# Seven products in the second layer of the last block of the second MLP, with GpSimd summing its weights

## The chip, the cores and the metric

The kernel runs on one core of a Trainium2 chip. The core has a matrix engine (TensorE, PE in the profile), three engines for elementwise work (VectorE, DVE; ScalarE, ACT; GpSimd, POOL) and a queue engine (SyncE, SP) that issues most transfers. The metric is the time of one execution in device microseconds, lower is better; the time before is the median of three runs.

## The reference

The program is three stages on 2304 tokens (4 sequences of 576) of 512 numbers. First comes attention with random features, then a mixer MLP (over tokens, then over channels), and then the stage that the change is in:

```python
X = np.fft.fft(np.fft.fft(x, axis=1), axis=2)
u = x + np.real(X)
un = (u - mean(u)) / np.sqrt(var(u) + 1e-06)      # over the 512 channels
return u + np.maximum(un @ w_ch1, 0.0) @ w_ch2    # 512 -> 2048 -> 512
```

All of it is in float32. The kernel keeps that precision with three matmuls in a reduced format (fp32r) for each product: each operand is split into a high part and a rest, and high x high, high x rest and rest x high are summed in PSUM. So every weight lies in memory twice, as a high part and as a rest (`kept`), and every activation is split by two operations, a copy on ScalarE (high) and a subtraction on VectorE (rest).

## The kernel before, in words

The second MLP runs over three blocks of token tiles of 128 rows: `PLAIN` (4 tiles), and the two of `PAIRED` with 6 and 8 tiles. The change is in the last one, c = 1, with 8 tiles, which are two halves of 4 tiles, that is of 512 tokens.

Layer one of a paired block (`paired_block`, first loop) takes the hidden units in 8 pairs of slabs (p_ = 0 to 7), each slab 128 hidden units. For a pair, the two token halves and the two halves of the 512 inputs make a 2 x 2 block product, and the kernel forms it with seven products (P1 to P7, each six matmuls of 512 columns in `product`, L1519) in place of eight, by sums of weights and of activations that are made beforehand. The products go into two PSUM banks X and Y in turn; VectorE and ScalarE combine them to four results: the hidden values of the two token halves for the two slabs. Those of the first token half are split at once and used; those of the second wait in SBUF (`held`).

Layer two multiplies the hidden values with `kept[2, p_]` in the plain way: `downs` gives 12 matmuls of 512 columns for a slab and a token half of 4 tiles. Within pass p_ the list `todo` holds the 24 matmuls of pass p_ - 1 for the first token half, and they are run in four groups between the products, so that TensorE has work while the other engines combine. After the eight passes the second token half follows, slab by slab (16 slabs, `part` splits a slab two ahead).

The order of every engine's work is the order in which the program issues it; a wait on one instruction holds what is behind it on the same engine. Weights come through `Slots` (six buffers w0 to w5 of 512 KB, `ffw`): SP fetches them in the order of the list `flow`, a fetch is issued when a buffer comes free, some five fetches ahead. `side` spreads other work (transforms and norms of later tiles) over TensorE's steps; by the last block it is empty. The sums of the first layer's weights are made the same way earlier (`sum_pairs`, on VectorE, stored by GpSimd's queue). Results are added to the rows in SBUF and sent out by `put_out` (L1275). `reopen` (L1507) runs once in block 0, when the transform's buffers are free, and opens the pool `g2` in their place. `prepare_ff` (L1347) makes the last block's activations and their sums between the slabs of block 0's second token half.

## Time and profile before

| | |
|---|---|
| median of three runs | 934.48 us (934.14 to 936.88) |
| the profiled execution | 934.46 us |
| its span in the trace | 932.7 us |
| TensorE busy | 923.9 us, 99% |
| VectorE, ScalarE, GpSimd busy | 638.1, 305.6, 134.4 us |
| granted TensorE clock | 0.999 |
| DMA | 214.36 MB, mean 230 GB/s |

The span is the time from the first to the last instruction; what the execution takes beyond it is start and end of the program. Busy time counts an engine's instructions, and overlapping matmuls count once. An engine that is busy for nearly the whole span need not be at its best rate: how far apart matmuls of one kind start says more, and a timeline shows that. The last block's passes begin at 760.8 us.

### The profile page before, as it was taken

How to read it: one execution, taken by the hardware profiler on the slowest of the kernel's cores; microseconds unless marked ns; L12 is line 12 of the kernel's file. 1: busy time of each engine (PE TensorE's matmuls, PEld its weight loads, DVE VectorE, ACT ScalarE, POOL GpSimd, SP SyncE). 2: the span in 40 equal slices, each digit the busy share in tenths (PEclk: the TensorE clock that was granted, in tenths of full speed). 3: DMA queues.
4: the chain of work that ended last, by engine and by line, in shares of the span. 5: the costliest groups of instructions: out<-in, count | busy, mean ns of one | idle time of the engine just before them, and what ended most of it. 6: DMA issues, size and time to landing. Idle time of an engine off the chain costs nothing.

```text
span 932.7 us, 13693 instructions
## 1 busy us (share of the span) xinstructions
PE 923.9 (99%) x5174; PEld 812.1 (87%) x5174; DVE 638.1 (68%) x1231; ACT 305.6 (33%) x697; POOL 134.4 (14%) x133
## 2 busy tenths in 40 slices
PE   8999999999999999999999999999999999999998
PEld 8999999988889888888888888889999888888886
DVE  6987999896775788876796795536666764333432
ACT  5886777742121222221222222221111251111220
POOL 3353444221211122101020001000000000000000
PEclk9999999999999999999999999999999999999999
DMA  8765564688996687595197958247765657566452
GB/s 278 231 213 177 180 220 160 242 305 318 329 420 259 240 297 268 197 337 189 54 371 298 327 190 289 84 160 247 242 218 184 216 197 229 181 199 196 159 193 100
DMA packets 61825, 214.36 MB, mean 230 GB/s; under 512 B 5568, under 2 KB 6208, under 8 KB 48064
## 3 DMA queue, kind: packets, MB, share of 16 engines
q1 hardware_dynamic: 51104, 153.52, 47.2%
q0 software_dynamic: 10512, 59.84, 17.6%
q8 instruction: 41, 0.67, 0.3%
q14 instruction: 24, 0.20, 0.1%
q10 hardware_dynamic: 144, 0.13, 0.0%
HBM read 167.20 MB, written 42.47 MB: 225 GB/s over the span
## 4 chain that ended last, share of the span: by engine, by line
PE 95%; DVE 2%; ACT 1%; DMA 1%; issue 0%; SPq 0%; DVEq 0%; ACTq 0%
PE H L786 20%; PE A L1538 16%; PE A L912 16%; PE H L1525 14%; PE A L1297 5%; PE A L511 5%; PE N L587 3%; PE H L545 3%; PE A L570 2%; PE A L690 2%; PE S L1094 2%; PE A L677 1%; PE S L1107 1%; PE S L690 1%; PE H L677 1%; PE S L677 1%
## 5 line engine op out<-in xcount | busy, mean ns | idle before, releaser
L786 PE MATMUL H<-uh,w 128*128 128x512 f32 (+1 forms) x608 | 188.0, 375 | 0.0
L786 PEld LDWEIGHTS H<-uh,w 128*128 128x128 f32 x608 | 111.9, 188 | 19.6
L874 ACT ACTIVATE hh<-H 128x512 fp32r<-128x512 f32 (+1 forms) x76 | 42.9, 565 | 237.8 <-PE H L786 232.8
L786 PE MATMUL H<-ul,w 128*128 128x512 f32 (+1 forms) x304 | 113.5, 373 | 0.4 <-DVE ul L773 0.4
L912 PE MATMUL A<-hh,w 128*128 128x512 f32 (+1 forms) x480 | 109.6, 371 | 0.0
L1525 PE MATMUL H<-b,w1t 128*128 128x384 f32 (+1 forms) x480 | 104.2, 363 | 0.0
L1525 PEld LDWEIGHTS H<-b,w1t 128*128 128x128 f32 x480 | 87.4, 188 | 11.5 <-DVE b L1338 0.4
L912 PEld LDWEIGHTS A<-hh,w 128*128 128x128 f32 x480 | 83.5, 189 | 14.6
L875 DVE SCALAR_TENSOR_TENSOR hl<-H,hh 128x512 fp32r<-128x512 f32 (+1 forms) x76 | 49.0, 645 | 61.7 <-ACT hh L874 61.5
L1538 PE MATMUL A<-w2t,hx 128*128 128x512 f32 x336 | 81.9, 392 | 0.0
L529 ACT ACTIVATE f<-A,mx 128x128 f32<-128x128 f32 x240 | 69.7, 397 | 23.3 <-DVE mx L525 22.8
L1538 PEld LDWEIGHTS A<-w2t,hx 128*128 128x128 f32 x336 | 62.5, 188 | 12.7
L786 PEld LDWEIGHTS H<-ul,w 128*128 128x128 f32 x304 | 57.3, 188 | 10.2 <-DVE ul L773 0.8
L912 PE MATMUL A<-hl,w 128*128 128x512 f32 (+1 forms) x240 | 59.2, 368 | 0.0
L912 PEld LDWEIGHTS A<-hl,w 128*128 128x128 f32 x240 | 42.6, 188 | 7.6
L525 DVE TENSOR_REDUCE mx<-A 128x4 f32<-128x512 f32 x70 | 47.5, 681 | 1.0 <-ACT f L529 0.9
L1538 PE MATMUL A<-w2t,hy 128*128 128x512 f32 x192 | 46.8, 389 | 0.0
L1538 PEld LDWEIGHTS A<-w2t,hy 128*128 128x128 f32 x192 | 36.0, 188 | 7.5
L545 PE MATMUL H<-v,f 128*128 128x65 f32 x320 | 40.2, 270 | 1.2 <-ACT f L533 0.8
L545 PEld LDWEIGHTS H<-v,f 128*128 128x128 f32 x320 | 38.9, 191 | 1.9 <-ACT f L533 1.0
L360 DVE SCALAR_TENSOR_TENSOR cvo<-cvy,cvo 128x1024 int32<-128x1024 int32 (+2 forms) x32 | 39.7, 1239 | 0.5
L364 DVE SCALAR_TENSOR_TENSOR cvo<-cvo,stg 128x1024 f32<-128x1024 int32 (+2 forms) x32 | 39.9, 1247 | 0.0
(278 smaller groups left out, 1712.4 us busy)
## 6 DMA issues: line engine op xcount, KB each, us to landing
w<-kept SPq DMA_DIRECT2D x50, 1024.0 KB, 7.3
w2t<-kept SPq DMA_DIRECT2D x55, 512.0 KB, 4.2
w1t<-kept SPq DMA_DIRECT2D x48, 512.0 KB, 4.6
stg<-in_wff_dram POOLq DMA_DIRECT2D x16, 1024.0 KB, 6.9
kept<-cvo POOLq DMA_DIRECT2D x13, 1024.0 KB, 7.4
stg<-in_wch_dram SPq DMA_DIRECT2D x9, 1024.0 KB, 6.4
kept<-cvo POOLq DMA_DIRECT2D x16, 512.0 KB, 8.1
sw<-kept POOLq DMA_DIRECT2D x8, 1024.0 KB, 7.8
```

The costliest lines, as they stand in the source:

```text
L364: dve.scalar_tensor_tensor(out=st["l"].bitcast(F32), in0=st["l"], scalar=2.0 ** 32, in1=st["lw"].bitcast(U32), op0=ALU.mult, op1=ALU.add)
L511: pe.matmul(out=pj[:, p_ * 256:p_ * 256 + 256], lhsT=a[:, c, :], rhs=w, start=(n == 0), stop=(n == 2), skip_group_check=True)
L525: dve.tensor_reduce(out=mx, in_=p4, axis=AX.X, op=ALU.max, negate=True)
L529: act.activation(out=f[:, hh], in_=p4[:, hh], func=AF.Exp, bias=mx[:, hh])
L545: pe.matmul(out=kvp[b, g][:, hh * 65:hh * 65 + 65], lhsT=ft["k", i, g][:, hh, :], rhs=src["v", i, int(off > 0)][:, 4 * g + hh, :], start=( ...
L786: pe.matmul(out=hb[:, 0:n], lhsT=w(a, kk), rhs=u[:, kk, 0:n], start=(c == 0), stop=(c == 11))
L874: act.activation(out=hh, in_=hb[:, 0:n], func=AF.Relu)
L875: dve.scalar_tensor_tensor(out=hl, in0=hb[:, 0:n], scalar=0.0, in1=hh, op0=ALU.max, op1=ALU.subtract)
L912: pe.matmul(out=acc[i][:, 0:cols], lhsT=a[:, cs], rhs=v, start=(n == 0 and c_ == 0), stop=(n == NCH - 1 and c_ == 2))
L1297: pe.matmul(out=acc[t], lhsT=a[:, t * 128:t * 128 + 128], rhs=w, start=(n == 0 and c_ == 0), stop=(n == NFF - 1 and c_ == 2))
L1525: pe.matmul(out=to, lhsT=w[:, a, cs], rhs=v[:, q], start=(start and n == 0), stop=(n == 5), skip_group_check=True)
L1538: pe.matmul(out=acc[t], lhsT=h[n // 2][:, t * 128:t * 128 + 128], rhs=w[:, n % 2], start=(begins and n == 0), stop=(ends and n == 2))
```

## The change

Layer two of the last block is formed with seven products as well. Its 2 x 2 block product has the two token halves on one side, the two halves of the 512 outputs on the other, and sums over the two slabs of a pair; so a matmul has 256 columns in place of 512, and a product is 12 of them.

- New weights: for each pair, `sums_of_second` loads `kept[2, p]` into SBUF, adds its two slabs and forms four sums or differences of 256 columns on GpSimd, copies the high part on ScalarE, subtracts the rest on GpSimd, and stores both as `kept[4, p]` from GpSimd's queue. The loads, sums and output have one buffer each (tags z0, z1, z2). `split(p)` (copy, rest, store, then the add of the next pair) is called at slabs 3 and 10 of block 0's second half for pairs 0 and 1, and in pass p_ of the last block for pair p_ + 2.
- Passes: the pass combines its products to values of seven operands. Three of the seven products of layer two (`a11`, `cd`, `f2_`) are put off to the next pass as before, 36 matmuls of 256 columns into three accumulators of two banks each. The values for the other four (K12, K3, K4, K22) stay in SBUF in `store`, 32 buffers of 128 x 512.
- After the passes, 32 steps of 12 matmuls take those four products, one after the other, over the eight pairs. Each accumulator is copied to SBUF between two of its uses (`snap`), and the copies are added to the rows in pieces of 256 columns.
- Fetches: of `kept[2, p]` and `kept[4, p]` in pieces of 256 columns, 256 or 512 KB per buffer.

```diff
--- before.py
+++ after.py
@@ -1468,16 +1468,31 @@
         for p_ in range(NP):
             due = due or [None, None]
             flow += [(1, p_, 0), due[0], (1, p_, 1), (1, p_, 2), due[1], (1, p_, 3)]
-            due = [(2, p_, 0), (2, p_, 1)]
+            due = [(5, p_, 0), (4, p_, 0)] if c else [(2, p_, 0), (2, p_, 1)]
         flow += due
+        if c:
+            flow += [(6, i, k) for i in range(4) for k in range(NP // 2)]
+            continue
         rest = [(2, p_, s_) for p_ in range(NP - 1, -1, -1) for s_ in (1, 0)]
         flow += rest[:-2]
         due = rest[-2:]
-    flow += due
...
+        if k > 3:
+            t = pl_.tile([128, 2, 2, 256], F32R, tag=tag, name="w3t")
+            v = t.bitcast(F32)
+            if k == 5:
+                sync.dma_start(out=v[:, 0], in_=kept[2, p_][:, :, 0:256])
+            elif k == 4:
+                sync.dma_start(out=v, in_=kept[4, p_][:, 0:4:3])
+            else:
+                for m in range(2):
+                    q = 2 * i + m
+                    sync.dma_start(out=v[:, m], in_=kept[4, q][:, (1, 2)[p_ // 2]] if p_ % 2 else
+                                   kept[2, q][:, :, 512 + 128 * p_:768 + 128 * p_])
+            return t
         if k == 2:
             t = pl_.tile([128, 2, 512], F32R, tag=tag, name="w2t")
             sync.dma_start(out=t.bitcast(F32), in_=kept[2, p_][:, :, i * 512:i * 512 + 512])
@@ -1489,7 +1504,7 @@
         return t
 
     def made(x):
-        return ((2, x[1]) if x[0] == 2 else (3, x[1])) in whole
+        return {1: (3, x[1]), 2: (2, x[1]), 4: (4, x[1]), 5: (2, x[1]), 6: (4, NP - 1)}[x[0]] in whole
 
...
@@ -1512,9 +1527,45 @@
         hx = xp.tile([128, 6 * n0], F32R, tag="x2", name="hx")
         ring.append([hx[:, n * n0:n * n0 + n0] for n in range(6)])
         hbuf.append([hx[:, n * n1:n * n1 + n1] for n in range(4)])
-        ring.append(hbuf[1])
-        v = [held5[:, n * n1:n * n1 + n1] for n in range(7)]
-        held.append(v + [g2.tile([128, n1], F32, name=f"t3_{n}") for n in range(2 * NP - len(v))])
+        store = [held5[:, n * n1:n * n1 + n1] for n in range(7)]
+        held.append(store + [g2.tile([128, n1], F32, name=f"t3_{n}") for n in range(4)])
+        sums_of_second(g2)
+    def sums_of_second(g2):
+        def load(p):
+            t = g2.tile([128, 2, 1024], F32, tag="z0", name="zw")
+            pool.dma_start(out=t, in_=kept[2, p])
+            return t
+        ws, ys = [], []
+        def add(p):
+            w = ws.pop(0)
+            y = g2.tile([128, 1024], F32, tag="z1", name="zy")
+            ys.append(y)
+            pool.tensor_tensor(out=y, in0=w[:, 0], in1=w[:, 1], op=ALU.add)
+            if p + 1 < NP:
+                ws.append(load(p + 1))
+            v = y.rearrange("p (c n) -> p c n", c=4)
+            for to, a, b in ((0, 1, 0), (1, 3, 1), (3, 3, 0), (2, 2, 3)):
+                pool.tensor_tensor(out=v[:, to], in0=v[:, a], in1=v[:, b], op=ALU.subtract)
+        def split(p):
+            y = ys.pop(0)
+            o = g2.tile([128, 2, 1024], F32R, tag="z2", name="zo")
+            act.copy(out=o[:, 0], in_=y)
+            pool.tensor_tensor(out=o[:, 1], in0=y, in1=o[:, 0], op=ALU.subtract)
+            kept[4, p] = dram.tile([128, 4, 2, 256], F32, name="kept4")
+            keep(pool, kept[4, p], o)
+            whole.add((4, p))
+            if p + 1 < NP:
+                add(p + 1)
+        ws.append(load(0))
+        add(0)
+        tmp["split"] = split
 
...
@@ -1552,9 +1603,6 @@
 
     def paired_block(c, todo, uses, after):
 
-        if c:
-            hy = fp.tile([128, 4 * n1], F32R, tag="t2_5", name="hy")
-            hbuf[1] += [hy[:, n * n1:n * n1 + n1] for n in range(4)]
...
@@ -1636,19 +1684,198 @@
                 run(mats)
                 ffw.used()
                 side.step(S_US)
+                if n in (3, 10):
+                    side.until(lambda: "split" in tmp, side.lead)
+                    tmp["split"](n // 7)
             else:
                 left += mats
         return left, 1, lambda: finish(c, 1, acc)
 
+    def last_block(todo, uses, after):
+        c, g2 = 1, right["n"]
+        hy = fp.tile([128, 4 * n1], F32R, tag="t2_5", name="hy")
+        hy = [hy[:, n * n1:n * n1 + n1] for n in range(4)]
+        parts = [hy[:2], hbuf[1][2:], hbuf[1][:2], hy[2:]]
+        sa, ub, vc, cd = temps(c)
+        left = [g2.tile([128, n1], F32, tag="un", name="ku", bufs=8) for _ in range(8)]
+        store = held[1] + left[:6]
+        f11, f2_ = left[6:]
+        kx = xu.tile([128, 4, n1], F32, tag="x2", name="kx", padded_shape=[128, 4, S])
+        store += [kx[:, n] for n in range(4)]
+        spare_ = []
+        def more():
+            ky = xp.tile([128, 4, n1], F32, tag="x2", name="ky", padded_shape=[128, 4, S])
+            z1 = g2.tile([128, 2, n1], F32, tag="z1", name="kz1")
+            z0 = g2.tile([128, 4, n1], F32, tag="z0", name="kz0")
+            z2 = g2.tile([128, 4, n1], F32, tag="z2", name="kz2")
+            v = [t[:, n] for t, m in ((ky, 4), (z1, 2), (z0, 4), (z2, 4)) for n in range(m)]
+            n = 4 * NP - len(store)
+            store.extend(v[:n])
+            spare_.extend(v[n:])
+        def kept_(p_, i):
+            return store[4 * p_ + i]
+        K12, K3, K4, K22 = range(4)
...
+        by_part = [(t, n) for n in range(3) for t in range(4)]
+        first = len(todo) // 2
+        late = None
+        for p_ in range(NP):
+            X, Y = [bank("H")[:, 0:n1] for _ in range(2)][::(1, -1)[p_ % 2]]
+            a11 = parts[p_ % 2]
+            w = ffw.get((1, p_, 0))
+            product(c, X, w[:, 0], P1, True)
+            act.copy(out=sa, in_=X)
+            product(c, Y, w[:, 1], P6, True)
+            combine(ub, Y, sa, ALU.add)
+            if late:
+                late()
+            ffw.used()
+            side.step(S_US)
+            run(todo, first // 2)
+            if p_ + 2 < NP:
+                tmp["split"](p_ + 2)
+            w = ffw.get((1, p_, 1))
+            product(c, X, w[:, 0], P2, False)
+            relu_parts(a11, X)
+            act.activation(out=f11, in_=X, func=AF.Relu)
+            product(c, Y, w[:, 1], P5, True)
+            combine(vc, Y, ub, ALU.add)
+            side.step(S_US)
+            run(todo, first - first // 2)
+            ffw.used(1 + uses)
+            w = ffw.get((1, p_, 2))
+            product(c, X, w[:, 1], P7, True)
+            combine(kept_(p_, K22), X, vc, ALU.add)
+            relu(kept_(p_, K22))
+            product(c, Y, w[:, 0], P3, False)
+            combine(vc, Y, ub, ALU.add)
+            relu(vc)
+            combine(kept_(p_, K3), f11, vc, ALU.subtract)
+            combine(cd, vc, kept_(p_, K22), ALU.add)
+            combine(f2_, cd, f11, ALU.subtract)
+            ffw.used()
+            side.step(S_US)
+            run(todo, len(todo) // 2)
+            two(parts[2], cd)
+            w = ffw.get((1, p_, 3))
+            product(c, X, w[:, 0], P4, False)
+            combine(kept_(p_, K12), X, ub, ALU.add)
+            relu(kept_(p_, K12))
+            side.step(S_US)
+            run(todo)
+            ffw.used(1 + uses)
+            two(parts[3], f2_)
+            late = lambda p_=p_: combine(kept_(p_, K4), kept_(p_, K12), f2_, ALU.subtract)
+            uses = 1
+            if p_ == 0:
+                after()
+                more()
+                acc1, acc2 = [[bank("A") for _ in range(2)] for _ in range(2)]
+                acc3 = [bank("S") for _ in range(2)]
+                first = 12
...
+            b, e = p_ == 0, p_ + 1 == NP
+            todo += (mats(acc1, a11, weights((5, p_, 0), 0), b, e, by_part)
+                     + mats(acc3, parts[2], weights((4, p_, 0), 0), b, e, by_part)
+                     + mats(acc2, parts[3], weights((4, p_, 0), 1), b, e, by_part))
+        late()
+        chain = [(K12, acc1), (K3, acc2), (K4, acc3), (K22, acc2)]
+        steps = [(i, p_) for i in range(4) for p_ in range(NP)]
+        def part(n):
+            i, p_ = steps[n]
+            h = parts[n % 4]
+            two(h, kept_(p_, chain[i][0]))
+            return h
...
+        m1, m6, m5, m8 = (sa, ub), (vc, cd), spare_[0:2], (spare_[2], f11)
+        at = {0: [lambda: snap(acc3, m5)], 1: [lambda: snap(acc2, m6)], 8: [lambda: snap(acc1, m8)],
+              16: [lambda: snap(acc2, m6)], 24: [lambda: snap(acc3, m5)]}
...
+        spread(2, adds(m5, 1, 256))
+        spread(3, adds(m6, 0, 256))
+        spread(8, adds(m1, 0, 256))
+        spread(10, adds(m8, 0, 0))
+        spread(12, adds(m1, 1, 256))
+        spread(14, adds(m1, 1, 0))
+        spread(18, adds(m6, 1, 256, (256, 512)))
+        spread(26, adds(m5, 0, 256, (0, 512)))
+        hs = {0: part(0)}
+        run(todo, 12)
+        snap(acc1, m1)
+        hs[1] = part(1)
+        run(todo)
+        ffw.used(2)
+        for n, (i, p_) in enumerate(steps):
+            if n + 2 < len(steps):
+                hs[n + 2] = part(n + 2)
+            end = n + 1 == len(steps)
+            run(mats(chain[i][1], hs.pop(n), weights((6, i, p_ // 2), p_ % 2), False, p_ + 1 == NP,
+                     [(t, k) for t in range(4) for k in range(3)] if end else by_part))
+            if p_ % 2:
+                ffw.used()
+            for fn in at.get(n, []):
+                fn()
+        act.copy(out=vc, in_=acc2[0])
+        for t in (0, 1, 3, 2):
+            x = place(1, t, 0)
+            src_ = (vc if t < 2 else acc2[1])[:, t % 2 * 256:t % 2 * 256 + 256]
+            combine(x, x, src_, ALU.add)
+            r = PAIRED[c][4 + t] * 128
+            sync.dma_start(out=out[r:r + 128, 0:256], in_=x)
     side.credit, side.most = 0.0, 2.0
     carry = [lambda q=q: parts_of(0, P4, q, late(1, q)) for q in range(2)], 0, None
-    for c in range(len(PAIRED)):
-        if c == 0:
-            side.lead += later_rows + sum(dft(3), []) + [(0.0, reopen)] + sum(norm(2), [])
-        carry = paired_block(c, *carry)
-    run(carry[0])
-    ffw.used(2)
-    carry[2]()
+    side.lead += later_rows + sum(dft(3), []) + [(0.0, reopen)] + sum(norm(2), [])
+    last_block(*paired_block(0, *carry))
```

## Rows read from the trace of the kernel before

**Rows 1.** The page: chain of waits, share of the span by engine.

```profile
PE 95%; DVE 2%; ACT 1%; DMA 1%; issue 0%; SPq 0%; DVEq 0%; ACTq 0%
```

**Rows 2.** TensorE timeline, last block: start us, length us, engine, line, operation, count.

```profile
884.88 5.60 PE L1538 MATMUL A<-w2t,hy 128*128 128x512 f32 x24
...
890.32 5.60 PE L1538 MATMUL A<-w2t,hx 128*128 128x512 f32 x24
```

**Rows 3.** Timeline of TensorE, channel block of 256 columns.

```profile
281.34 1.12 PE L912 MATMUL A<-hh,w 128*128 128x256 f32 x8
...
284.22 1.12 PE L912 MATMUL A<-hh,w 128*128 128x256 f32 x8
```

**Rows 4.** Timeline of all engines, one pass of the last block.

```profile
792.40 1.52 PE L1538 MATMUL A<-w2t,hx 128*128 128x512 f32 x6
...
792.67 0.69 DVE L1573 TENSOR_TENSOR tmp<-H,tmp 128x512 f32<-128x512 f32 x1 [2.07 <-PE H L1525]
...
795.32 0.60 ACT L1530 ACTIVATE hy<-H 128x512 fp32r<-128x512 f32 x1 [3.44 <-PE H L1525]
...
795.95 0.69 DVE L1531 SCALAR_TENSOR_TENSOR hy<-H,hy 128x512 fp32r<-128x512 f32 x1 [2.59 <-ACT hy L1530]
...
807.63 0.69 DVE L1573 TENSOR_TENSOR tmp<-H,tmp 128x512 f32<-128x512 f32 x1 [2.06 <-PE H L1525]
```

**Rows 5.** Timelines of GpSimd and VectorE, where the two meet.

```profile
142.91 1.31 POOL L499 TENSOR_TENSOR ql<-qs,qh 128x512 fp32r<-128x512 f32 x1 [5.22 <-ACT qh L497]
...
143.43 1.87 DVE L360 SCALAR_TENSOR_TENSOR cvo<-cvy,cvo 128x1024 int32<-128x1024 int32 x1
...
144.53 1.91 POOL L619 TENSOR_TENSOR xl<-x,xh 128x512 fp32r<-128x512 f32 x1 [0.32 <-ACT xh L618]
...
159.19 1.22 DVE L360 SCALAR_TENSOR_TENSOR cvo<-cvy,cvo 128x1024 int32<-128x1024 int32 x1
...
197.42 1.52 POOL L619 TENSOR_TENSOR xl<-x,xh 128x512 fp32r<-128x512 f32 x1 [3.09 <-issue]
...
197.70 0.45 DVE L693 TENSOR_TENSOR x<-A,x 128x288 f32<-128x288 f32 x1
```

**Rows 6.** Groups by line: busy us, mean ns of one, idle before.

```profile
L1254 ACT CAST so<-cvy 128x1024 fp32r<-128x1024 f32 x8 | 8.4, 1051 | 17.7 <-DVE cvy L1248 17.7
...
L421 POOL DMA_DIRECT2D kept<-so x16 | 12.1, 757 | 50.0 <-DVE so L1258 30.7 <-ACT so L1254 9.0 <-ACT sh L1054 9.0
...
L1234 POOL DMA_DIRECT2D sw<-kept x8 | 4.4, 548 | 76.2 <-DVE cvy L1239 70.3 <-DVE cvo L364 5.8
```

**Rows 7.** Timelines of ScalarE, VectorE, TensorE where the last block begins.

```profile
753.92 0.59 ACT L1365 COPY tmp<-S 128x512 f32<-128x512 f32 x1 [1.01 <-PE S L1344]
...
759.04 0.55 DVE L1531 SCALAR_TENSOR_TENSOR hx<-t,hx 128x384 fp32r<-128x384 f32 x1
...
760.80 3.18 PE L1525 MATMUL H<-b,w1t 128*128 128x512 f32 x12
...
761.91 1.29 DVE L1338 TENSOR_TENSOR b<-tmp,b 128x512 fp32r<-128x512 f32 x2
...
763.83 1.08 PE L1538 MATMUL A<-w2t,hx 128*128 128x512 f32 x4
```

**Rows 8.** DMA: us to landing (480.7 and 481.5 second), then stretches with share, GB/s.

```profile
kept<-so POOLq DMA_DIRECT2D x16, 512.0 KB, 9.3
...
DMA to landing us min/median/max: 11.4/12.4/13.3
...
480.00:500.00 20.00, 20.00 (x102) 16.97 (x102) 14.62 (x31) 6.11 (x11) 4.11 (x6) 1.00 1.01 393
...
800.00:880.00 80.00, 80.00 (x355) 66.24 (x354) 26.03 (x39) 10.08 (x17) 0.00 (x0) 1.00 0.58 189
```

**Rows 9.** Timeline of the end.

```profile
928.60 0.76 DVE L1280 TENSOR_TENSOR L<-A,L 128x256 f32<-128x256 f32 x2
```

**Rows 10.** Group by line: weight loads beside 256 and 512 columns.

```profile
L912 PEld LDWEIGHTS A<-hh,w 128*128 128x128 f32 x480 | 83.5, 189 | 14.6
```

More of the change, by code (lines that the diff above doesn't have):

```diff
@@ L1641, in paired_block, with relu, two, combine @@
         return left, 1, lambda: finish(c, 1, acc)
+    def last_block(todo, uses, after):
[22 more added lines that the diff above has]
+        K12, K3, K4, K22 = range(4)
+        def relu(t):
+            act.activation(out=t, in_=t, func=AF.Relu)
+        def two(h, src):
+            act.copy(out=h[0], in_=src)
+            dve.tensor_tensor(out=h[1], in0=src, in1=h[0], op=ALU.subtract)
+        def combine(out_, a, b, op):
+            dve.tensor_tensor(out=out_, in0=a, in1=b, op=op)
+        def mats(acc, h, w, begins, ends, order_):
+            def one(t, n):
+                b, cs = t // 2, slice(t % 2 * 256, t % 2 * 256 + 256)
+                pe.matmul(out=acc[b][:, cs], lhsT=h[n // 2][:, t * 128:t * 128 + 128], rhs=w()[:, n % 2],
+                          start=(begins and n == 0 and t % 2 == 0), stop=(ends and n == 2), skip_group_check=True)
+            return [lambda x=x: one(*x) for x in order_]
+        by_part = [(t, n) for n in range(3) for t in range(4)]
[55 more added lines that the diff above has]
+                first = 12
+            def weights(x, m):
+                return lambda: ffw.get(x)[:, m]
+            b, e = p_ == 0, p_ + 1 == NP
[10 more added lines that the diff above has]
+            return h
+        def snap(acc, to):
+            for a, t in zip(acc, to):
+                act.copy(out=t, in_=a)
+        def place(h, t, lo):
+            return row(PAIRED[c][4 * h + t])[:, lo:lo + 256]
+        def adds(to, h, lo, then=None):
+            def one(t):
+                x = place(h, t, lo)
+                combine(x, x, to[t // 2][:, t % 2 * 256:t % 2 * 256 + 256], ALU.add)
+                if then:
+                    r = PAIRED[c][4 * h + t] * 128
+                    sync.dma_start(out=out[r:r + 128, then[0]:then[1]], in_=row(r // 128)[:, then[0]:then[1]])
+            return [lambda t=t: one(t) for t in range(4)]
+        m1, m6, m5, m8 = (sa, ub), (vc, cd), spare_[0:2], (spare_[2], f11)
+        at = {0: [lambda: snap(acc3, m5)], 1: [lambda: snap(acc2, m6)], 8: [lambda: snap(acc1, m8)],
+              16: [lambda: snap(acc2, m6)], 24: [lambda: snap(acc3, m5)]}
+        def spread(n, fns):
+            for k, fn in enumerate(fns):
+                at.setdefault(n + k, []).append(fn)
+        spread(2, adds(m5, 1, 256))
[29 more added lines that the diff above has]
+            sync.dma_start(out=out[r:r + 128, 0:256], in_=x)
```

## The prediction

> **What bounds the kernel now.** I read the page first: TensorE holds 95% of the chain of waits, and no other engine more than 2% [rows 1], so time can only come from TensorE's own work, or be lost by making it wait. Next I read the timeline of TensorE for the price of a matmul by width. In the last block 24 matmuls of 512 columns start 5.44 us apart [rows 2]: 226.7 ns each. The short channel block has matmuls of 256 columns, each with its own weights as in the change; 24 of them take 2.88 us [rows 3]: 120.0 ns each. Half the columns cost 53%, not 50%. Then I read all engines over one pass of the last block: it lasts 14.96 us [rows 4], which is 66 x 226.7 ns, so nothing but matmuls is in it. Last I looked for what GpSimd does to VectorE, since the change gives GpSimd its first arithmetic since the attention stage [rows 5].
>
> **TensorE's work.** Before, each of the 8 passes has 42 matmuls of layer one and puts off 24 of layer two to the next pass; 16 slabs of 12 follow. After, a pass puts off 36 matmuls of 256 columns (three of the seven products), and 32 steps of 12 follow (the other four). Layer two goes from 384 x 226.7 ns = 87.04 us to 672 x 120.0 ns = 80.64 us: **-6.40 us**. By place: seven passes go from 14.96 to 42 x 226.7 + 36 x 120 ns = 13.84 us (-7.84), and what follows the last pass from 216 x 226.7 ns = 48.96 to 420 x 120 ns = 50.40 us (+1.44).
>
> By the Trainium skill (TensorE: Matmul & The Clock Gate, Back-to-back issue gap), columns over 2.4 GHz plus 2.5 ns part two matmuls, which is 109 and 216 ns. By it this work would save 9.5 us; rows 2 and 3 show 120.0 and 226.7, and the measurement decides.
>
> **The new work of VectorE and ScalarE in a pass.** An operation on 128x512 takes about 0.69 us on VectorE and 0.6 on ScalarE, VectorE follows ScalarE by 0.03 us, and either starts some 0.26 us after TensorE's last issue [rows 4]. I count from the start of P1 (six matmuls are 1.36 us; the put-off groups are 0.72, 0.72, 1.44 and 1.44). Two points could stop TensorE. P7, at 6.88, overwrites the bank that a11's rest is made from: P2 ends at 4.80, ScalarE's relu at 5.65, VectorE's rest at 6.37, so 0.5 us is spare. The next pass's P6, at 15.20, overwrites the bank that K12 reads: P3 ends at 9.60, vc at 10.56, its relu at 11.2, then K3, cd, f2 and the rest of cd in a row on VectorE to 13.9, K12 at 14.5: 0.7 spare. VectorE's 12 operations fill 8 us of 13.84. Alone they cost nothing, and no other gap is smaller.
>
> **GpSimd's sums.** A subtraction of 128x512 takes it 1.31 us [rows 5]; 1024 and 256 columns are in no row, and I scale: 2.62 and 0.66 (with a fixed part of 0.2 us in the 1.31 it would be 2.4 and 0.76). Per pair: add, four subtractions, one subtraction of the rest, two stores of 0.757 and a load of 0.548 to issue [rows 6]: 2 x 2.62 + 4 x 0.66 + 1.51 + 0.55 = 9.9 us of a pass of 13.84. It keeps up. But rows 5 show what it does to others: VectorE's operation with two SBUF inputs, issued at 143.43 inside a GpSimd one, ends at 145.30, 1.22 us (its time alone) after about 144.1, where GpSimd's ends; the next GpSimd one, issued at 144.53, ends 1.3 us after VectorE's. The two take turns, each for a whole instruction. VectorE's operation with one PSUM input is untouched (0.45 us at 197.70, inside GpSimd's). In a pass K4, K3, cd, f2 and two rests have two SBUF inputs.
>
> The Trainium skill (GPSIMD Engine Reference, Specifications) says that SBUF interfaces are shared and contended by VectorE instructions with two SBUF inputs. Rows 5 agree for scalar_tensor_tensor; a plain tensor_tensor beside GpSimd is in no row.
>
> I walk a pass with that. ScalarE's 1.05 us copy of the sums follows sa and ends near 3.4; GpSimd's rest holds the port from 3.45 to 6.0. K4, due at 3.6, ends near 6.6, a11's rest behind it at 7.1, not 6.37: P7 waits 0.3 us. Stores, the next add and the load take GpSimd to 10.7; its four subtractions then alternate with K3, cd, f2 and the rest of cd, each waiting up to 0.6: K12 ends 1 to 1.5 us late, less 0.7 spare and 0.3 already lost: 0 to 0.5. Together **0.6 us** per pass; 0 if plain tensor_tensor does not take turns, 1.4 at the 0.2 us fixed part. The passes with sums are p=0 to 5; I charge 0.6 to p=2 to 5 (**+2.4**), and to p=1, where the chain still runs late, **+0.9** (0 to 2).
>
> **The boundary between the blocks.** Before, TensorE already waits 0.3 us there: 12 matmuls from 760.80 would end at 763.52, the next start at 763.83, because VectorE's rest of P6 ends at 763.2 [rows 7]. ScalarE's copy of pair 1 fits the 1.01 us it idles before 753.92. Then GpSimd's rest (754.0 to 756.6), stores, the add (758.1 to 760.7) and four subtractions (761.2 to 763.9) meet VectorE's last rests: the one at 759.04 waits 1.5 us, those of P5 and P6 take turns with the subtractions, and some idle time absorbs part. I take **+2.0 us** (0 to 3) for TensorE in pass 0.
>
> **Transfers.** A pass fetches 2.62 MB for TensorE (189 GB/s); stores and loads of the sums add 2.1 MB, some 330 GB/s in all. The window 480 to 500 reached 393 GB/s with all DMA engines busy, the last block now uses 0.58 of them at 189 [rows 8]. Fetches run five slots, some 10 us, ahead, so I take 0; half a microsecond per pass if they come late. SP's fetch of a pair's sums waits for their store and holds the fetches behind it, but it is issued more than a pass after the store: 0. The kept values go to buffers that were last read long before. After the last pass GpSimd is done; each step of 1.44 us asks VectorE for 0.69 plus at most two 0.4 us adds [rows 9], with parts two steps ahead: 0. Its fetches are 182 GB/s, half in 1 KB pieces; no row prices these, and even half again of the 0.58 stays under 1: 0.
>
> **The end.** Now two 0.38 us adds of 256 columns follow the last matmul [rows 9]; then up to four, as the two copied ones come out of ScalarE only about then: **+0.5 us** (0 to 0.8).
>
> **Sum.** -6.4 + 0.5 + 2.0 + 0.9 + 2.4 = -0.6 us. The profiled execution took 934.46 us (span 932.7 and 1.8 around it), the median is 934.48: **933.9 us**. No change means within 2.8 us (0.3%), what a measurement of this kernel can tell.
>
> **Rivals.**
> 1. *VectorE and GpSimd do not get in each other's way where it counts* (tensor_tensor needs no turns, or GpSimd's operations fall into VectorE's 5.5 us of idle time). For it: the spare 0.5 and 0.7 us, and that most operations read PSUM. Against: rows 5. Then -6.4 + 0.5 = 928.6 us; with half the turns, 931.
> 2. *Slower: the store holds ScalarE.* The sums have one output buffer, so ScalarE's copy of the next pair waits until the store has landed, and the relus behind it on ScalarE wait too, then TensorE. The loop is copy 1.05 + rest 2.62 + issue 0.76 + landing, so it decides from a landing of 9.4 us in a pass of 13.84. The median landing is 9.3 us, and a pair stored behind a load took 11.4 to 13.3 [rows 8]; here no load is right ahead of the pair, which speaks for 7 to 8. At 11 us a pass takes 15.4, at 12 us 16.4: with the 2.0 at the boundary and the 0.5 at the end, six passes give 934.5 - 6.4 + 2.5 + 6 x 1.6 = 940 and 946 us.
> 3. *Slower: GpSimd's operations take longer than scaled* (1.4 us per pass, 3 at the boundary, 2 in p=1): 934.5 - 6.4 + 0.5 + 3 + 2 + 4 x 1.4 = 939 us.
> 4. *Weights bind.* A weight load is listed at 189 ns [rows 10]; at that pace layer two would take 127 us, 974 us in all. Rows 3 load weights for each matmul at 120 ns: 1 in 100.
>
> **Chances.** Forecast (931.7 to 937.3) 0.39; rival 1 and halves of it 0.31; rivals 2, 3 and 4 together 0.30. The range leaves out 1 in 10 on either side: 928.5 to 941; the forecast's own is 931.7 to 937.3.
>
> **What would show it.** The 256-column matmuls of layer two at 120 ns; passes of 14.2 to 15 us in p=2 to 5 and 13.84 in p=6 and 7; VectorE's K4 or cd lines over 1 us where they cross GpSimd; TensorE waiting for VectorE at P7 and P6, not for a DMA. Passes of 13.84 throughout would show rival 1, ScalarE waiting for a landing rival 2. The forecast falls if a 256-column matmul in that pattern is not 120 ns, or if TensorE waits for fetched weights.

## The result, and the profile after

The changed kernel takes 941.97 us (median of 5 runs, 939.88 to 942.32) against 934.48 (5 runs): ratio 1.0068, 95% interval 1.0051 to 1.0086. It is slower; the forecast was 933.9, with no change the likeliest. The profiled execution is the median one, 941.97 us with a span of 939.8 (before 932.7).

The chain of waits of the changed kernel, beside [rows 1]: TensorE's share has fallen from 95% to 80%. Only a part of that fall is time lost. About half of it lies between 410 and 490 us, in code that the change doesn't touch: the chain passes there by GpSimd's queue and a store, while TensorE is busy without a break (74.00 of the 74 us from 413 to 487, in both kernels). What was lost is read from TensorE's own waits.

```profile
PE 80%; DVE 8%; issue 7%; DMA 3%; ACT 1%; POOL 0%; SPq 0%; DVEq 0%; ACTq 0%; POOLq 0%
```

TensorE's waits in the changed kernel (who waits on what: us in total, times, longest). The same view of the kernel before lists none of these.

```profile
PE H L1576 <- DVE t L1732: 2.4, 2, 1.4
PE H L1576 <- DVE ku L1732: 1.9, 2, 1.5
...
PE H L1576 <- DVE b L1338: 1.6, 1, 1.6
...
PE A L1737 <- DVE U L1280: 0.6, 1, 0.6
```

`t` and `ku` on L1732 are K12: P6 of the next pass overwrites the bank that K12 reads. `b` on L1338 is a part of P6's operand at the boundary of the blocks, `U` block 0's last rows.

Where they stand, on TensorE's timeline (start us, length us, engine, line, operation, count, and in brackets the idle time before and what ended it): pass 0, as [rows 7]; P1 and P6 of pass 4; P7 of pass 6 (the weight load, PEld, last); the last block's layer two, as [rows 2].

```profile
762.37 2.20 PE L1576 MATMUL H<-b,w1t 128*128 128x512 f32 x9
764.89 0.50 PE L1576 MATMUL H<-b,w1t 128*128 128x512 f32 x1 [0.32 <-ACT b L1337]
766.94 0.74 PE L1576 MATMUL H<-b,w1t 128*128 128x512 f32 x2 [1.55 <-DVE b L1338]
...
825.27 1.55 PE L1576 MATMUL H<-b,w1t 128*128 128x512 f32 x6
828.32 1.65 PE L1576 MATMUL H<-b,w1t 128*128 128x512 f32 x6 [1.50 <-DVE ku L1732]
...
862.32 0.87 PE L1737 MATMUL A<-w3t,hx 128*128 128x256 f32 x6
863.17 1.66 PE L1576 MATMUL H<-buh,w1t 128*128 128x512 f32 x6
863.17 1.22 PEld L1576 LDWEIGHTS H<-buh,w1t 128*128 128x128 f32 x6 [0.18 <-ACT ku L1762]
...
887.31 3.04 PE L1737 MATMUL A<-w3t,hy 128*128 128x256 f32 x24
890.19 3.04 PE L1737 MATMUL A<-w3t,hx 128*128 128x256 f32 x24
```

24 matmuls of 256 columns take 2.88 us, 120.0 ns each, as forecast. P7's matmuls at 863.17 are listed without a wait, but six matmuls of 120 ns from 862.32 end at 863.04: TensorE stood for 0.13 us. Its weight load waited for ScalarE's L1762, which takes f11 from P2's bank, and began only with the matmul, so P7 then took 0.14 longer (1.66 us for six against 1.52). That 0.14 is the restart spoken of below.

Pass 3, from 809.88, on VectorE, ScalarE and GpSimd, as [rows 4, 5]: K3, cd, f2 and the rest of cd stand in a row from 822.61, and K12, for which P6 of pass 4 waits, comes at 827.59.

```profile
816.79 0.69 DVE L1582 SCALAR_TENSOR_TENSOR hx<-H,hx 128x512 fp32r<-128x512 f32 x1 [1.37 <-ACT hx L1581]
817.52 0.60 ACT L1762 ACTIVATE ku<-H 128x512 f32<-128x512 f32 x1 [0.76 <-DVE hx L1582]
...
822.61 1.62 DVE L1732 TENSOR_TENSOR ku<-ku,tmp 128x512 f32<-128x512 f32 x1 [0.70 <-ACT tmp L1725]
822.91 4.21 POOL L1553 TENSOR_TENSOR zy<-zy 128x256 f32<-128x256 f32 x4
824.15 1.22 DVE L1732 TENSOR_TENSOR tmp<-tmp,ku 128x512 f32<-128x512 f32 x1
825.41 1.12 DVE L1732 TENSOR_TENSOR ku<-tmp,ku 128x512 f32<-128x512 f32 x1
826.45 1.21 DVE L1729 TENSOR_TENSOR hx<-tmp,hx 128x512 fp32r<-128x512 f32 x1
827.59 0.68 DVE L1732 TENSOR_TENSOR ku<-H,tmp 128x512 f32<-128x512 f32 x1
```

The four with both inputs in SBUF take 1.1 to 1.6 us beside GpSimd's four subtractions, those that read a bank (`H`) 0.68 or 0.69 as before. Plain tensor_tensor takes turns too. The second thing to see is f11: ScalarE's L1762 begins 0.04 us after VectorE's rest of a11 has ended, with no need of its result. Both read the same bank, and the kernel makes the one wait for the other (the 0.76 us in the brackets).

The sums, transfers and end, beside [rows 5, 8, 9]: GpSimd's groups by line (busy us, mean ns), the stores' median time to landing, the stretch 760 to 880 (last two figures: share of the DMA engines, GB/s), and VectorE's last additions.

```profile
L1553 POOL TENSOR_TENSOR zy<-zy 128x256 f32<-128x256 f32 x32 | 28.6, 893 | 2.1
L1559 POOL TENSOR_TENSOR zo<-zy,zo 128x1024 fp32r<-128x1024 f32 x8 | 21.1, 2637 | 44.7 <-ACT zo L1558 44.7
L1548 POOL TENSOR_TENSOR zy<-zw 128x1024 f32<-128x1024 f32 x8 | 20.1, 2515 | 8.5 <-DMA zw<-kept 8.5
...
kept<-zo POOLq DMA_DIRECT2D x16, 512.0 KB, 5.8
...
760.00:880.00 120.00, 113.02 (x590) 94.39 (x589) 75.64 (x100) 44.32 (x74) 63.12 (x53) 1.00 0.82 280
...
934.93 0.76 DVE L1732 TENSOR_TENSOR U<-U,tmp 128x256 f32<-128x256 f32 x2 [4.46 <-ACT tmp L1867]
935.61 0.41 DVE L1732 TENSOR_TENSOR L<-L,A 128x256 f32<-128x256 f32 x1
```

The span grew by 7.1 us. From P1 to P1, and set against the forecast:

| stretch | forecast | measured |
|---|---|---|
| up to the last block's P1 (760.80, 762.37) | 0 | +1.57 |
| TensorE's work in the passes, at 120.0 ns | -7.84 | -7.84 |
| stalls: pass 0 (16.08 us) | +2.0 | +2.16 |
| pass 1 (16.94, less 13.84) | +0.9 | +3.10 |
| passes 2 to 5 (14.49, 15.39, 15.96, 14.88) | +2.4 | +5.36 |
| passes 6 and 7 (14.16 each) | 0 | +0.64 |
| after the last pass (55.37, before 53.27) | +1.94 | +2.10 |
| sum | -0.6 | +7.1 |

In the first row 1.24 us stand already before block 0, in code that the change doesn't touch. Block 0 begins at 623.4 us before and 624.6 after, and between 622.2 and 624.9 in the profiles of all the experiments but the third, so executions differ by that much there. The other 0.3 us are in block 0.

### The profile page after: what moved, and what is told of

The parts are those of the page before. It is cut to its first block, busy times and chain, and to the rows that moved or that the text cites. A ratio compares the mean times of both kernels' runs of the same rounds, so it can differ in the third digit from the quotient of the medians.

```text
span 939.8 us, 14662 instructions
## 1 busy us (share of the span) xinstructions
PE 922.2 (98%) x5462; PEld 820.5 (87%) x5462; DVE 692.8 (74%) x1314; ACT 351.2 (37%) x774; POOL 218.7 (23%) x205
## 4 chain that ended last, share of the span: by engine, by line
PE 80%; DVE 8%; issue 7%; DMA 3%; ACT 1%; POOL 0%; SPq 0%; DVEq 0%; ACTq 0%; POOLq 0%
PE H L786 17%; PE H L1576 13%; PE A L912 12%; PE A L1589 6%; PE A L1737 5%; PE A L1297 5%; PE A L511 4%; PE N L587 3%; PE H L545 3%; PE S L1737 2%; DMA kept<-so 2%; PE A L677 1%; PE A L570 1%; PE S L1094 1%; PE A L690 1%
## 5 line engine op out<-in xcount | busy, mean ns | idle before, releaser
L1576 PE MATMUL H<-b,w1t 128*128 128x384 f32 (+1 forms) x480 | 106.6, 366 | 6.2 <-DVE t L1732 2.4
L499 POOL TENSOR_TENSOR kl<-ks,kh 128x512 fp32r<-128x512 f32 x16 | 22.7, 1416 | 72.6 <-ACT kh L497 64.1
L348 ACT ACTIVATE cvy<-cvy 128x1024 f32<-128x1024 f32 (+2 forms) x32 | 32.8, 1026 | 16.6 <-DVE cvy L341 16.6
L1737 PE MATMUL A<-w3t,hy 128*128 128x256 f32 x288 | 38.4, 283 | 0.6 <-DVE U L1280 0.6
L1737 PEld LDWEIGHTS A<-w3t,hy 128*128 128x128 f32 x288 | 37.1, 191 | 2.0 <-DVE U L1280 0.8
```

The source lines that it names most:

```text
L1576: pe.matmul(out=to, lhsT=w[:, a, cs], rhs=v[:, q], start=(start and n == 0), stop=(n == 5), skip_group_check=True)
L1737: pe.matmul(out=acc[b][:, cs], lhsT=h[n // 2][:, t * 128:t * 128 + 128], rhs=w()[:, n % 2], start=(begins and n == 0 and t % 2 == 0), stop ...
```

## The experiments

Each was timed beside the kernel before on the same chip (medians 934.4 to 935.5), and the ratios are to that. The changed kernel was not timed again with them, so differences to its 941.97 carry about 1 us from chip to chip. The first four take one thing away or move it.

**1. GpSimd's arithmetic left out** (its loads and stores stay; what is stored is a copy of the loaded weights, not the sums).

```diff
-            pool.tensor_tensor(out=y, in0=w[:, 0], in1=w[:, 1], op=ALU.add)
-                pool.tensor_tensor(out=v[:, to], in0=v[:, a], in1=v[:, b], op=ALU.subtract)
-            pool.tensor_tensor(out=o[:, 1], in0=y, in1=o[:, 0], op=ALU.subtract)
```

> Left out: GpSimd's add, four subtractions and rest of every pair; the stored values are the loaded ones, so kept[4] is not the sums. Copies on ScalarE, loads, stores and all else stay. Theory 1 (GpSimd and VectorE take turns, which makes VectorE's last rests at the boundary and K12 in the passes late): TensorE's waits at P6 go, pass 0 falls from 16.1 to about 13.9 us, passes 1 to 5 from 14.5 - 16.9 to about 14.2, in all 9 us less than the changed kernel's 942: 933. Theory 2 (stores and loads hold ScalarE or the fetches): no change, 941 to 943. Theory 3 (the order of operations on VectorE and ScalarE is itself too slow): passes 1 to 5 stay above 14.5, 940 to 942.

Measured: 936.07 us, ratio 0.9998 (0.9983 to 1.0014). All waits for K12 and at the boundary are gone and the passes from 2 on take 14.16 to 14.22 us. So GpSimd's arithmetic costs about 6 us by being there. The 933 already counted 14.2 us for a pass; it is missed in pass 1, which takes 16.85. There 0.61 us go for block 0's rows as in the changed kernel, and at its end stands a wait for a fetch that the changed kernel does not have (TensorE, then SyncE's queue):

```profile
792.93 2.97 PE L1564 MATMUL H<-b,w1t 128*128 128x512 f32 x12 [1.39 <-DMA w1t<-kept]
```

```profile
780.07 0.34 SPq L1281 DMA_DIRECT2D out_dram<-U  x1
...
781.70 1.00 SPq L1503 DMA_DIRECT2D w1t<-kept  x1
```

The fetch at 781.70 feeds P1 of pass 2. SyncE has it behind block 0's three stores, which wait for VectorE's additions; P1 starts 11.2 us after its issue.

**2. Loads and stores of pairs 1 to 7 left out** (arithmetic as in the change, on pair 0's values).

> Left out: the loads and stores of pairs 1 to 7 of the sums; GpSimd works on pair 0's weights again, and all pairs' fetches read pair 0's stored sums. The arithmetic stays. Theory 1 (turns): the waits stay, 940 to 943, at most 1 to 2 us better, since GpSimd's run per pair gets 2 us shorter and its subtractions start earlier in the pass. Theory 2 (transfers): back to about 933.

Measured: 936.51, ratio 1.0016 (1.0004 to 1.0028), 3.5 us below the least that theory 1 gave. But it is not the transfers that held TensorE (1 has them all, at 936.07): without GpSimd's time to issue them its add comes 2 us earlier in the pass, so the four subtractions meet operations that read a bank and K12 is on time; now GpSimd's rest stands in front of K4 (2.73 us on VectorE instead of 0.68), a11 and f11 come late behind it, and P7 waits 0.55 us in the passes 2 to 5 (pass 2, GpSimd and VectorE):

```profile
795.15 2.42 POOL L1558 TENSOR_TENSOR zo<-zy,zo 128x1024 fp32r<-128x1024 f32 x1 [6.25 <-ACT zo L1557]
...
795.39 2.73 DVE L1733 TENSOR_TENSOR t<-t,ku 128x512 f32<-128x512 f32 x1
```

The same arithmetic costs what it happens to meet.

**3. Only the four 256-column subtractions left out.**

> Left out: only the four subtractions of 256 columns per pair (3.2 to 4.2 us of GpSimd each); add, rest, copies and transfers stay. If the four that alternate with K3, cd, f2 and the rest of cd make K12 late: the waits at P6 of passes 1 to 5 go, some 5 us, and part of the boundary's 2.2 us: 935 to 936.5. If the long ones (add and rest, 2.4 to 3 us) hold VectorE most: under 2 us better, 940 or more.

Measured: 936.75, ratio 1.0010 (0.9999 to 1.0020). Of the 6 us, 5 are these four small operations: the waits for K12 are gone, P7's 0.47 to 0.56 appear instead as in 2. The waits are read from an execution of 944.72 us, whose excess lies in the first 100 us, where the granted clock was 0.93.

**4. K12 early**: on VectorE, K12 goes ahead of f2, the rest of cd, and K3.

```diff
+            combine(cd, vc, kept_(p_, K22), ALU.add)
...
+            product(c, X, w[:, 0], P4, False)
+            combine(kept_(p_, K12), X, ub, ALU.add)
+            relu(kept_(p_, K12))
             combine(f2_, cd, f11, ALU.subtract)
             two(parts[2], cd)
+            combine(kept_(p_, K3), f11, vc, ALU.subtract)
```

> Nothing left out. In each pass K12 is formed on VectorE right behind cd, ahead of f2, the rest of cd and K3. Theory 1: K12 then waits behind one operation that takes turns and not behind four, the waits at P6 in passes 1 to 5 go (1.4, 1.0, 1.5 and 0.4 us, and some 0.14 at each restart), about 4.5 us: 937 to 938. If something else sets P6 (the landing of a fetch, ScalarE's queue): 941 to 943.

Measured: 938.02, ratio 1.0037 (1.0018 to 1.0056): 3 to 4 us back by order alone. TensorE then waits for the next thing in line, the second fetch of pass 2 and f11 at P7 of pass 3:

```profile
797.36 2.99 PE L1576 MATMUL H<-b,w1t 128*128 128x512 f32 x12 [1.28 <-DMA w1t<-kept]
...
815.69 1.65 PE L1576 MATMUL H<-buh,w1t 128*128 128x512 f32 x6 [0.43 <-ACT ku L1762]
```

**5. f11 first**: f11 from the bank, and a11 cut from f11 instead of from the bank.

```diff
-            relu_parts(a11, X)
             act.activation(out=f11, in_=X, func=AF.Relu)
+            two(a11, f11)
```

> Nothing left out. ScalarE writes f11 straight from the bank, ahead of a11, and a11 is cut from f11 in SBUF; so the bank that P7 writes is free without VectorE. Theory 1 (P7 waits 0.13 us, and 0.14 for the restart, in every pass because f11 stands behind VectorE's subtraction for a11): the passes 6 and 7 go from 14.16 to 13.9, pass 0 gains the same; passes 1 to 5 gain nothing where P6 goes on waiting for K12, since VectorE's work is as long as before: 0.8 to 2.2 us less than the changed kernel, 939.8 to 941.2, and the trace shows no wait of P7 for ScalarE. Theory 2 (14.16 is the rate of TensorE itself with 672 matmuls of 256 columns): passes 6 and 7 stay at 14.16 and the time at 942.

Measured: 942.93, ratio 1.0083 (1.0064 to 1.0102): no gain, against theory 1. Passes 6 and 7, without GpSimd, do go to 13.92, so f11 is the cause of the 14.16. But a11's rest now has both inputs in SBUF, and beside GpSimd it takes up to 3.73 us instead of 0.69. VectorE's line and GpSimd's in pass 2, and what TensorE does then (P3 overwrites the bank whose sum stands behind a11's rest on VectorE):

```profile
804.77 3.73 DVE L1729 TENSOR_TENSOR hy<-ku,hy 128x512 fp32r<-128x512 f32 x1
805.44 2.51 POOL L1548 TENSOR_TENSOR zy<-zw 128x1024 f32<-128x1024 f32 x1
...
809.16 2.93 PE L1576 MATMUL H<-bul,w1t 128*128 128x512 f32 x6 [2.31 <-DVE tmp L1732]
...
807.00:813.00 6.00, 3.84 (x14) 3.26 (x15) 3.49 (x4) 0.78 (x2) 4.46 (x6) 0.72 1.01 328
```

The six matmuls after the wait take 2.93 us instead of 1.65; the granted clock in 807 to 813 is 0.72 (third figure from the end), that is, part of it at 1.2 GHz instead of 2.4.

**6. The early split**: GpSimd's second split two slabs earlier in block 0.

```diff
-                if n in (3, 10):
+                if n in (3, 8):
```

> Nothing left out. GpSimd's second split and the sums of pair 2 are issued two slabs earlier in block 0 (after slab 8 instead of 10), so that VectorE's subtractions for the first operands of the last block stand clear of them. Theory 1 (the 1.9 us of waits at the start of pass 0, 0.32 for ScalarE and 1.55 for VectorE, are VectorE's turns with GpSimd beside the operands of P6): they go, pass 0 takes 14.2 instead of 16.1, the rest as in the changed kernel: 940. Theory 2 (the boundary is held by the fetches and stores there, a DMA share of 0.93): the wait gets another name and the time stays at 941.5 to 942.5.

Measured: 944.0, ratio 1.0090 (1.0074 to 1.0106). The waits of pass 0 do go, but two subtractions of operands before them stand behind GpSimd (2.50 and 3.88 us) and hold block 0 for longer (VectorE's second, TensorE, and the stretch after):

```profile
754.26 3.88 DVE L1338 TENSOR_TENSOR b<-tmp,b 128x512 fp32r<-128x512 f32 x1
...
759.69 1.30 PE L1589 MATMUL A<-w2t,hx 128*128 128x512 f32 x3 [3.42 <-DVE hx L1582]
...
761.00:766.00 5.00, 5.00 (x22) 4.17 (x22) 3.90 (x7) 1.05 (x3) 1.28 (x2) 0.75 0.76 267
```

**7. K12 early, f11 first and the early split together.**

> Nothing left out. K12 early on VectorE (as in the run with K12 early, 938.0), f11 first, and the early split, in one kernel. Theory 1 (three orders of work, each with its own wait, that add up): 938.0 less 1.9 at the boundary, less 0.43 to 0.57 in the passes 3 to 5 and 0.13 to 0.27 in the others, in all 934.0 (932.5 to 935.5), with passes from 3 on at 13.85 to 13.95 and the waits of pass 1 left (0.7 for the bank, 1.3 for a fetch). Theory 2 (GpSimd's turns cost VectorE a fixed time for each pass that comes out somewhere whatever the order): 937 to 939, with the waits under another name. Before is 934.5 to 934.9.

Measured: 947.77 (940.77 to 952.47), ratio 1.0126 (1.0087 to 1.0166): far from the 934. Both harms of 5 and 6 are in it: a11's rest takes 3.6 us and P3 waits up to 2.1 us for the sum behind it, and the 3.4 us in block 0 are there. The spread goes with the clock: the execution of 952.2 us has a mean granted clock of 0.988, that of 940.8 one of 0.999.

**8. As 7, with block 0's three stores behind the next fetch and their additions ahead of f2's parts.**

```diff
+            while p_ and puts:
+                puts.pop(0)()
...
+            if p_ == 0:
+                after(puts)
             two(parts[3], f2_)
```

> Nothing left out. The three edits, and block 0's last three rows are added to on VectorE ahead of f2's parts, with their three stores issued behind the next fetch instead of ahead of it. Theory 1 (the wait of 1.3 us for the first fetch of pass 2 is SyncE's: the stores wait there for VectorE's additions, and the fetch stands behind them): the fetch is issued some 2.5 us earlier, its wait goes, and the 0.6 to 0.7 us for the bank shrinks by half or more: 1.6 us less than the kernel with three edits, about 932.4 (931 to 934), faster than before by 0.2%. Theory 2 (that fetch is late because the transfers are dense there, 0.93 of their engines): issued earlier it lands as late, the same time as with three edits within 0.4 us.

Measured: 947.75, ratio 1.0125 (1.0104 to 1.0145), the same as 7. The wait for block 0's rows is gone, but kernel 7 has no wait for the fetch to start with, so it tells nothing of the stores. All six executions have a granted clock of 0.994 to 0.996, so part of the time is the clock's.

In these eight VectorE is stretched where it meets GpSimd's arithmetic, and moving GpSimd's work only changed what it met (6, 7). So the next took the arithmetic off GpSimd without losing it.

**9. The sums on VectorE**, in its idle times (the remarks in the cut say where).

```diff
-            pool.tensor_tensor(out=y, in0=w[:, 0], in1=w[:, 1], op=ALU.add)
+            dve.tensor_tensor(out=y, in0=w[:, 0], in1=w[:, 1], op=ALU.add)
...
+            adds_(p_ + 2)      # after K4
...
+            sums_(p_ + 2)      # the four, after P5's sum
...
+            high_(p_ + 2)      # ScalarE, after vc's relu
...
+            low_(p_ + 2)       # after K12
```

> Nothing left out. The sums, the four subtractions and the low parts are made by VectorE instead of GpSimd, put into four of its rests in each pass (after K4, after the sum of P5's bank, after K12) and in block 0 after one slab each; GpSimd only issues transfers. VectorE gets some 4.1 us more per pass (1.3 for the sum, 1.4 for the four, 1.3 for the low part, from its 0.69 us for 512 columns), 12.4 of 13.84. Theory 1 (what stretches VectorE is standing behind whole GpSimd instructions whenever it reads two operands from SBUF, and that alone): without GpSimd the passes come to 14.1 to 14.3 as with the arithmetic left out, and the time to 936 to 938 in spite of the added work. Theory 2 (VectorE is full; GpSimd's share of the work has to be paid somewhere): 943 or more, with waits for K12 or f11 of 0.5 us and more in each pass. Theory 3 (transfers): 941 to 943, since every load and store is as before.

Measured: 937.28, ratio 1.0021 (1.0002 to 1.0039). Theory 1: 4.7 us below the change (4.4 by the ratios) with more work on VectorE, and from pass 2 on passes of 14.16, the same as with no arithmetic at all. Pass 0 grew to 17.39, by waits at P6 that 10 has too, and by the clock: 0.50 from 767 to 770. An operation that GpSimd did in 2.4 us takes VectorE 1.22.

**10. As 9, with f11 right behind a11's high part and block 0's additions and stores as in 8.**

```diff
-            relu_parts(a11, X)
+            act.activation(out=a11[0], in_=X, func=AF.Relu)
             act.activation(out=f11, in_=X, func=AF.Relu)
+            dve.scalar_tensor_tensor(out=a11[1], in0=X, scalar=0.0, in1=a11[0], op0=ALU.max, op1=ALU.subtract)
```

> Nothing left out. The sums on VectorE; f11 taken from the bank right behind a11's high part, so that ScalarE does not stand behind VectorE's low part; the last three rows of block 0 added to ahead of f2's parts, their stores issued behind the next fetch. Theory 1: 0.13 us of wait for f11 and 0.14 for the restart go in each of 8 passes (2.2), and in pass 1 the wait for the bank (0.6) and the fetch (1.4): 936.5 less 4.0, about 932.5 (931 to 934.5), passes of 13.85 to 13.95, faster than before. Theory 2 (passes of 14.1 are TensorE's own rate here): 935 to 936.5.

Measured: 934.96, ratio 0.9997 (0.9979 to 1.0015), above the 932.5. The passes came to 14.02: P7's bank is free 0.06 us before P7, but not early enough for its weights to be loaded ahead (VectorE's rest of a11 and P7's weight load, pass 4; P7 takes 1.65 us):

```profile
827.72 0.69 DVE L1770 SCALAR_TENSOR_TENSOR hy<-H,hy 128x512 fp32r<-128x512 f32 x1 [0.74 <-ACT ku L1769]
...
828.47 1.22 PEld L1581 LDWEIGHTS H<-buh,w1t 128*128 128x128 f32 x6
```

And 2.1 us went at the boundary, where VectorE makes pair 1's sums and low part among the operands of P6 (VectorE, ScalarE, TensorE):

```profile
752.76 1.80 DVE L1558 TENSOR_TENSOR zy<-zy 128x256 f32<-128x256 f32 x4
...
754.80 1.05 ACT L1562 CAST zo<-zy 128x1024 fp32r<-128x1024 f32 x1 [2.62 <-DMA kept<-zo]
...
766.00 0.50 PE L1581 MATMUL H<-b,w1t 128*128 128x512 f32 x1 [1.08 <-ACT b L1340]
```

ScalarE's copy of pair 1 is listed as waiting 2.62 us for the store of pair 0 to land, which looks like rival 2 of the prediction. But the sums that it copies end only at 754.56, so the store holds it for 0.24 us at most. In 9 the copy waits for VectorE's sums and no store, and TensorE stands as long (ScalarE, TensorE):

```profile
753.52 1.05 ACT L1559 CAST zo<-zy 128x1024 fp32r<-128x1024 f32 x1 [2.46 <-DVE zy L1555]
...
764.71 0.50 PE L1578 MATMUL H<-b,w1t 128*128 128x512 f32 x1 [1.14 <-ACT b L1337]
```

So pair 1's work on VectorE, with the copy behind it, holds the boundary, and not the store. 12 moves all of it away.

**11. The change, with f11 as in 10 only.**

> Nothing left out; GpSimd as in the changed kernel. Only ScalarE's f11 is put right behind a11's high part, both from the bank, and VectorE's low part after them still reads the bank and not SBUF. Theory 1 (the earlier run with f11 first lost because its subtraction for a11 then read two operands from SBUF, 3.6 us instead of 0.69 beside GpSimd): here that subtraction stays at 0.69 and P7 no longer waits; K12's waits in the passes 1, 3, 4 and 5 stay: 0.5 to 1.0 us less than the changed kernel, 941 to 941.5, passes 6 and 7 at 13.9. Theory 2 (whatever moves ScalarE's reading of the bank makes VectorE late): 943 or more, as with f11 first.

Measured: 941.34, ratio 1.0073 (1.0049 to 1.0096), as theory 1 had it, though 0.6 us is within the spread; passes 6 and 7 take 14.02 instead of 14.16. Here a11's rest reads a bank and takes 0.69 us in every pass, where in 5 it took up to 3.73.

**12. As 10, each pair one pass later, and the 12 put-off matmuls around P2 and P5 divided 4 and 8 instead of 6 and 6.** The cut is against 10; the buffers of z0 are also taken for kept values before those of z1.

```diff
-                if 3 <= n < 11:
+                if 3 <= n < 7:
...
-            adds_(p_ + 2)
+            adds_(p_ + 1)
...
-            run(todo, first // 2)
+            run(todo, first // 3)
```

> Nothing left out. As the kernel with the sums on VectorE and the orders mended, with two edits. Pair 1 is not split in block 0 any more but in pass 0, and so on: each pair one pass later. And of the 12 matmuls ahead of and behind P2 and P5, 4 and 8 stand there instead of 6 and 6. Theory 1 (the kernel with the orders mended lost 2.0 to 2.3 us at the start of the last block, since ScalarE waited 2.6 us there for a store of pair 1 to land and VectorE made its low part among the first operands; and 0.14 us per pass because P7 finds its bank free just too late for its weights to be loaded ahead): both go: 935.0 less 2.0 and less 1.1, about 932 (930.8 to 933.5), ratio to before 0.9965 to 0.998. Theory 2 (the start of the last block is held by VectorE and ScalarE as such): 933.9 by the passes alone. Theory 3 (a pair's fetch now comes too soon after its store): a wait for w3t shows and the time is 935 or more.

Measured: 931.17 us (930.79 to 932.22), ratio 0.9962 (0.9948 to 0.9975): faster than before, and 10.8 us below the change (9.9 by the ratios). TensorE's P1 of the passes 3 and 4, the layer two after them, and VectorE's sums of a pair in pass 2 (add, four subtractions):

```profile
804.39 2.91 PE L1581 MATMUL H<-b,w1t 128*128 128x512 f32 x12
...
818.31 2.91 PE L1581 MATMUL H<-b,w1t 128*128 128x512 f32 x12
...
876.87 3.04 PE L1742 MATMUL A<-w3t,hy 128*128 128x256 f32 x24
...
795.03 1.22 DVE L1551 TENSOR_TENSOR zy<-zw 128x1024 f32<-128x1024 f32 x1
...
797.60 1.79 DVE L1558 TENSOR_TENSOR zy<-zy 128x256 f32<-128x256 f32 x4
```

Passes of 13.92 us from pass 2 on, 13.94 in pass 0: by place, the first edit ended the loss at the boundary, and the second that at P7, whose bank is now free 0.30 us ahead. Only pass 1 is still long (15.09), with 0.51 us for a sum behind block 0's additions.

## Why the prediction was wrong

- **TensorE's work** was right: 120.0 ns for a matmul of 256 columns, 420 of them in a row after the last pass, no weight-load bound. The last layer-two matmul ends 50.4 us after the passes, the 420 x 120.0 ns forecast.
- **Turns of VectorE and GpSimd** were the right mechanism, and their price is the step that failed: "each waiting up to 0.6: K12 ends 1 to 1.5 us late, less 0.7 spare and 0.3 already lost: 0 to 0.5. Together 0.6 us per pass". The 0.7 spare was about right. But K3, cd, f2 and the rest of cd lost 0.96, 1.87, 2.41 and 1.36 us together in the passes 1 to 4; in pass 3 they take 5.17 us instead of 2.76. Three of them waited 0.43 to 0.53 there, within the 0.6. K3 waited 0.93, though by the profile it was issued 0.3 us before the first subtraction. And the 0.3 "already lost" was not lost: when K12 is late, K4 comes before GpSimd's rest. So P6 came 0.3, 1.1, 1.7 and 0.6 us late in the passes 2 to 5, with a restart of 0.14 in three of them. That is 4.2 of the 5.36 us; most of the other is f11 (below). Experiments 3, 4 and 9 show K12's share from three sides. Where K12 is on time the walk came true: in 2 K4 starts 3.62 us after P1 (walked: 3.6) and ends at 6.35 (6.6) behind GpSimd's rest, and P7 waits.
- **GpSimd's durations.** A 256-column operation takes it 0.80 us alone (3.19 for four, in 2), not the 0.66 scaled; the 1024-column ones take 2.4 to 2.5, not 2.62. And of rows 5 the text misreads one figure: the next GpSimd operation ends 1.14 us after VectorE's (146.44 and 145.30), not 1.3. The sum does not use it.

By the Trainium skill (SBUF — State Buffer, Summary: rules for kernel authors), a VectorE operation with two SBUF inputs and a GpSimd operation that reads SBUF block each other whole, the second to issue until the first has finished. The rows of pass 3 agree for plain tensor_tensor, but for K3, which waits though it was the first to start by the profile. 5 against 11 shows the other half: the same subtraction, 3.73 us from SBUF and 0.69 from a bank.

- **P7** was walked with a11's rest as the last reader of its bank, 0.5 us to spare. The last is f11, 0.6 us after it, a term that the prediction put at nothing. That step failed in every pass but the first; passes 6 and 7, forecast at 13.84, show its 0.27 us, and 5, 11 and 12 bring them to 13.92, 14.02 and 13.92. That the 0.27 is near the 0.3 us that the prediction gave P7, for K4 behind GpSimd's rest, is luck.

The Trainium skill (PSUM — Partial Sum Buffer, PSUM bank collisions raise a hardware error) says that ScalarE and VectorE may not touch one bank together, reads included. That is the order that the trace shows for f11; that it must be so no run here tries.

- **Pass 1** (+0.9 forecast, +3.10): 1.42 for K12, 0.61 for block 0's rows, 0.17 for f11, and restarts behind each. The forecast had K12 alone.
- **The boundary** (+2.0 forecast, +2.16) was right in size and place: beside GpSimd's subtractions VectorE's two rests for P6 take 2.34 us, 1.29 before [rows 7]:

```profile
762.62 3.71 POOL L1553 TENSOR_TENSOR zy<-zy 128x256 f32<-128x256 f32 x4
...
764.54 2.34 DVE L1338 TENSOR_TENSOR b<-tmp,b 128x512 fp32r<-128x512 f32 x2
```

- **Transfers** at 0 were right for this kernel: the stores land in 5.8 us, no wait of TensorE names a fetch, the DMA engines are at 0.82. Without K12's wait fetches are late: by 0.58 us in block 0 and 1.39 for P1 of pass 2 in 1, by 1.28 for P2 of pass 2 in 4. That block 0's stores ahead on SyncE are to blame was argued, not shown: 9 has them ahead too, and no such wait.
- **The end** (+1.94 forecast, +2.10) was right.
- **Rivals.** Rival 3, GpSimd longer than scaled, came nearest (939): it had the 3 us at the boundary, 2 in pass 1 and 1.4 per pass where 2.16, 3.10 and 1.34 came. In part that is luck: of GpSimd's operations only the small ones take longer than scaled, and 0.27 of the 1.34 is f11. Rival 2 did not come: ScalarE's copies wait for no store in the change, and for 0.24 us at most in 10. Rivals 1 and 4 are out.

The time lies just beyond the range's 941.0: 6.0 of the 8.1 us missed are stalls in the passes, 1.6 stand ahead of the last block, most of them ahead of anything that the change touches.

## What to carry to other kernels

Before giving GpSimd elementwise work, list VectorE's operations with two SBUF inputs in the same stretch: each can stand behind a whole GpSimd instruction, and a chain of four behind four. Where VectorE has idle time, do the work there: it cost 1.22 us instead of 2.4 and stretched nothing, which turned 941.97 us into 937.28. It still stands in VectorE's line, so it has to be kept away from operands that TensorE is about to need (10 against 12). When walking a pass, follow the last reader of each bank, on whatever engine, and leave a margin: a bank free 0.06 us ahead still cost 0.14 us, since the weights were not loaded ahead (10), one free 0.30 us ahead cost nothing (12).
